# Tying the v maxima and the first weight pass to their emission places, and emitting loads and stores one slot later, in an attention and mixture-of-experts kernel

## The chip, the cores and the metric

One core of one Trainium2 chip runs the whole kernel. The metric is device time in microseconds (us), the median of three runs. TensorE has two clock levels, 1.2 and 2.4 GHz; the profile prints the granted clock as a share of full speed, so 0.5 is the lower level.

## The reference, cut to what matters

Inputs are q, k, v of shape (4 batches, 12 heads, 448 positions, 64), float32; w_in (768 x 2048) and w_out (2048 x 768), float64; and phi (768 x 32), w1 and w2 (8 experts, 768 x 1024 and 1024 x 768) of a second, soft mixture, float32.

```
scores = q k^T / 8, causal mask, softmax (denominator + 1e-9), times v
x = attention output as (1792 tokens, 768)
h = x @ w_in ; g = max(0.01 h, h) ; y = g @ w_out            # first mixture
logits = y @ phi ; d = column softmax ; c = row softmax       # second mixture
slots = d^T y ; per expert: relu(slots w1) w2 ; out = c @ slots_out
```

## The kernel before, in words

**Stages.** The work on attention goes by pairs of heads: 24 pairs n, six to a batch (NP = 6), each in three slots (`attention_slots`, L507). Slot 1 of pair n multiplies P by v for pair n-1 (`attend`, L417, tile O), lowers the maxima, and starts the scores of n; slot 2 has the inverses of the sums (`inverses`, L428, tile rs); slot 3 has `columns` (L452), the last scores, and the transposes of q and k for pair n+2 (`qk_stacks`, L331, tile qkps). `stage` (L736) runs slots: stage 0 has 21 (pairs 0 to 6, attention alone), and three stages of 18 follow, in which one column of g per slot is computed for the batch before (`up`, L583: 18 matmuls into H, then Prelu on ACT, L625). Batches 0 and 1 store g to DRAM (L627). What comes after stage 3 (from some 486 us) is the rest of batch 3, the logits, and the second mixture, whose weights are read from DRAM.

**Weights.** w_in and w_out come as doubles, 16 units each, and are turned into float32 by hand. `load_raw` (L153) loads raw words into a ring of raw buffers (3 in stages 0 to 2, 2 in stage 3; BUFS, L150). `to_f32` (L184) makes two first passes on ACT, Abs of the high word into t (L195) and its Sign into sg (L196), then for w_in a maximum on DVE (L198), and two integer passes on DVE (L199 shifts, L200 reads the low word and t); L200 is the last reader of the raw buffer. After it `load_raw` is called at once, so that the next unit's load is emitted there. t has a ring of 3 in stages 1 and 2, sg of 2. `prep_in` (L207) then finds a scale (`pow2_scale`, L106), and makes two half-precision parts on ACT and POOL (L214 to L224). `prep_out` (L225) multiplies by the sign on POOL (L231), stores the result to DRAM (wsc, L233) and transposes it on TensorE (wt_ps, wp_ps, wf_ps). Units 0 to 5 of w_in are in stage 0, 6 to 15 in stage 1, ten units of w_out in stage 2, the last six in halves in stage 3, spread over the first slots of a stage by `prep_start` (L273).

**v.** `load_v(n)` (L309) loads one pair's v into a ring of VRING = 7; `reduce_v(n)` (L319) takes its absolute maximum on DVE (L325), and after a batch's sixth one, a scale of the batch follows, which `columns` reads. In slot 3 of pair n the kernel emits `load_qk(n + 4)`, `load_v(n + 6)` and `reduce_v(n + 5)`, in this order. v of pair n + 6 takes the buffer that `attend(n - 1)` has read in slot 1 of pair n.

**What sets the order.** TensorE's order is written out: `in_order` (L97) puts each matmul behind the last one emitted. The order on DVE, ACT, POOL and SP (the queue that issues all DMAs) is chosen by the framework when the program is built: it simulates the engines, and on each one takes the instruction of highest priority among those whose inputs are there in the simulation. Priority follows emission, attention 300 places ahead (AHEAD, L740). An instruction whose input comes early in the simulation can so be put far ahead of its place of emission. On the chip each engine then runs its list strictly in order. `tc.issue_after(i)` adds an edge by which what is emitted under it is put behind i on i's engine; raw loads have had one already, behind the last q, k or v load (`last_load`, L164).

Of the kernel before, what the change touches and what calls it, by code (L numbers as in the profile page):

```python
# [10 lines left out]
F32 = mybir.dt.float32  # L11
# [23 lines left out]
def tile_attn_moe_softmoe(ctx: ExitStack, tc: tile.TileContext, q, k, v, w_in, w_out, phi, w1, w2, out, dbg=None):  # L35
    nc = tc.nc
# [55 lines left out]
    chain = [None]  # L92

    def last_tensor():
        return next(i for i in reversed(nc.cur_bb.bb.instructions[-80:]) if i.engine == mybir.EngineType.PE)

# [87 lines left out]
    def to_f32(u, absmax=None):  # L184
# [9 lines left out]
        ti = t.bitcast(I32)  # L194
        nc.scalar.activation(t, hw.bitcast(F32), AF.Abs, scale=2.0**-112)  # L195
        nc.scalar.activation(sg, hw.bitcast(F32), AF.Sign)  # L196
# [3 lines left out]
        nc.vector.scalar_tensor_tensor(ti, lw, 29, ti, ALU.logical_shift_right, ALU.bitwise_or)  # L200
        load_raw()
        return t, sg

    w_in32 = w_in.bitcast(I32)
# [20 lines left out]
    def prep_out(us):  # L225
# [3 lines left out]
        for u in us:  # L229
            wo, sg = to_f32(u)  # L230
            nc.gpsimd.tensor_tensor(wo, wo, sg, ALU.mult)  # L231
            c0 = DH * (u[2] or 0)
            nc.sync.dma_start(  # L233
                wsc.rearrange("(k g a p) n -> k a g p n", k=4, g=4, a=4)[f // 4, f % 4][:, :, c0 : c0 + wo.shape[1]], wo
            )
            yield
# [82 lines left out]
    def reduce_v(n):  # L319

        b, hp = divmod(n, NP)
        if hp == 0:
            v_am[b] = am = const.tile([128, NP + 1], F32, tag="v_am", bufs=2, name=f"v_am{b}")
            nc.vector.memset(am, 0.0)
        nc.vector.tensor_reduce(v_am[b][:CP, hp : hp + 1], v_t[n], AX.XY, ALU.max, apply_absolute_value=True)  # L325
        if hp == NP - 1:
            am = v_am[b]
            nc.vector.tensor_reduce(am[:, NP:], am[:, :NP], AX.X, ALU.max)
            s_v[b], inv_v[b] = pow2_scale(am[:, NP:], f"v{b}")
# [177 lines left out]
    def attention_slots():  # L507
# [10 lines left out]
        for n in range(NPAIR + 1):  # L518
# [14 lines left out]
            if here:  # L533
                weights(n, 1)
            yield
            if n > 0:
# [5 lines left out]
            if n + 2 < NPAIR:  # L542
                qk_stacks(n + 2)
                if n + 4 < NPAIR:
                    load_qk(n + 4)
            if n + NP < NPAIR:
                load_v(n + NP)
            if NP <= n + NP - 1 < NPAIR:
# [187 lines left out]
    def stage(slots, count, columns_of_g=None):  # L736

        had = started[0]
        for x in range(slots):
            with tc.high_priority(offset=AHEAD):  # L740
                next(slots_of_attention, None)
                if columns_of_g is not None and x not in GAPS:
                    next(columns_of_g)
# [296 lines left out]
```

## Time and profile before

| what | us |
|---|---|
| median of three runs | 719.35 |
| lowest, highest | 716.97, 721.56 |
| the profiled execution, and its span | 717.05, 715.3 |
| PE busy (share of span) | 606.0 (85%) |
| DVE, ACT, POOL busy | 354.8, 289.8, 232.2 |
| mean granted clock of TensorE | 0.938 |

The span is the time from the first to the last instruction. PE is TensorE's matmuls, DVE is VectorE, ACT is ScalarE, POOL is GpSimd, SP the queue of DMAs. A busy share is a mean over stages that have different limits; the windows below split it. L12 is line 12 of the kernel; all ordered matmuls have the line of their helper, L99, and are told apart by the tile that they write.

### The profile page before, as it was taken

To read this page: it belongs to the slowest core of one execution; us is meant where nothing else is said; L and a number is where in the kernel's file an instruction comes from. 1 tells how busy PE (TensorE), PEld (TensorE's weight loads), DVE (VectorE), ACT (ScalarE), POOL (GpSimd) and SP (SyncE) were. 2 spreads that over 40 slices of the span, in tenths; PEclk is the share of its full clock that TensorE was granted. 3 is DMA by queue.
4 is the path that set the end of the run, shared out by engine and by line. 5 is a ranking of instruction groups with operands and counts; after the bars stand their busy time and mean duration, and the time that the engine had idled before them with its cause. 6 is when DMAs were issued, how large, how long until landed. Compare 5 with 4: busy or idle time off the path is not lost.

```text
span 715.3 us, 12308 instructions
## 1 busy us (share of the span) xinstructions
PE 606.0 (85%) x4836; PEld 337.4 (47%) x4836; DVE 354.8 (50%) x884; ACT 289.8 (41%) x571; POOL 232.2 (32%) x247
## 2 busy tenths in 40 slices
PE   2888759997988799979799999999998996998544
PEld 2555535554544455546455555554343444454114
DVE  5787645677774446355326666534646423001004
ACT  1677543566764446445245555441122112011003
POOL 4468733567656333335113443331000000000000
PEclk9999977999899899979989999999999998899797
DMA  9933165454345335542213522201989435999967
GB/s 185 260 97 78 40 172 140 110 166 133 114 130 149 127 117 153 151 133 65 78 53 102 152 68 67 68 23 57 378 331 376 154 105 223 426 424 424 423 270 308
DMA packets 102449, 125.67 MB, mean 176 GB/s; under 512 B 69240, under 2 KB 91256, under 8 KB 98296
## 3 DMA queue, kind: packets, MB, share of 16 engines
q1 hardware_dynamic: 102392, 124.89, 52.6%
q8 instruction: 38, 0.62, 0.3%
q14 instruction: 19, 0.16, 0.1%
HBM read 105.74 MB, written 19.14 MB: 175 GB/s over the span
## 4 chain that ended last, share of the span: by engine, by line
PE 49%; DMA 18%; DVE 15%; ACT 8%; issue 4%; POOL 3%; SPq 2%; DVEq 0%; ACTq 0%; POOLq 0%
PE H L99 21%; DMA w<-in_moe_w_dram 8%; PE O L99 6%; DMA v<-in_v_dram 5%; PE T L99 4%; PE g_acc L99 3%; DVE g_nat L565 2%; DVE rs L440 2%; DVE junk L362 2%; PE ph L898 2%; PE qkps L99 2%; DMA raw_i_None<-in_moe_w_in_dram 2%; PE L L99 2%; ACT mr L374 1%; PE wt_ps L99 1%
## 5 line engine op out<-in xcount | busy, mean ns | idle before, releaser
L99 PE MATMUL H<-x,w 128*128 128x448 f16 x1152 | 235.7, 360 | 6.1 <-ACT g L625 6.1
L99 PEld LDWEIGHTS <-w 128*128 128x128 f16 x1152 | 110.6, 100 | 123.7 <-issue 33.3
L362 DVE CUSTOM_DVE_ANT_0 junk<-S,mask 112x448 bf16<-112x448 f32 (+1 forms) x192 | 84.6, 441 | 69.6 <-PE S L99 67.2
L402 POOL TENSOR_SCALAR_AFFINE_SELECT P<-P 112x448 f32<-112x448 f32 x48 | 30.6, 637 | 154.1 <-ACT P L398 154.1
L625 ACT ACTIVATE g<-H,iv 128x448 f32<-128x448 f32 x58 | 36.6, 631 | 102.4 <-PE H L99 95.2
L398 ACT ACTIVATE P<-T 112x672 f32<-112x672 f32 (+1 forms) x72 | 56.9, 790 | 24.8 <-PE T L99 24.6
L99 PE MATMUL T<-qkt 64*112 64x336 f32 (+3 forms) x576 | 60.3, 322 | 5.1 <-ACT P L398 4.4
L99 PE MATMUL O<-P,v 112*64 112x448 f32 (+3 forms) x384 | 58.2, 449 | 5.1 <-POOL P L402 4.7
L440 DVE RECIPROCAL rs<-rs 128x224 f32<-128x224 f32 x36 | 53.3, 1521 | 6.8 <-ACT rs L438 6.8
L99 PEld LDWEIGHTS T<-qkt 64*112 64x112 f32 x576 | 45.8, 187 | 13.7 <-ACT P L398 5.6
L411 POOL TENSOR_TENSOR tsum<-tsum,P 112x448 f32<-112x448 f32 (+1 forms) x48 | 44.8, 934 | 2.6
L99 PEld LDWEIGHTS O<-P,v 112*64 112x64 f32 x384 | 27.6, 151 | 34.7 <-issue 16.5
L374 ACT ACTIVATE mr<-mps,own 128x112 fp32r<-128x112 f32 x96 | 26.0, 354 | 43.7 <-PE mps L99 43.7
L986 PE MATMUL po<-w,hz 128*32 128x384 f32 x256 | 27.5, 551 | 18.2 <-DMA w<-in_moe_w_dram 18.2
L99 PE MATMUL S<-qkt 64*112 64x448 f32 (+1 forms) x192 | 34.0, 395 | 9.2 <-DVE mxe L362 7.3
L407 POOL TENSOR_TENSOR tsum<-P 112x672 f32<-112x672 f32 x24 | 40.1, 1672 | 1.8
L565 DVE STREAM_TRANSPOSE g_nat<-g 128x448 f32<-128x448 f32 x26 | 16.5, 639 | 45.5 <-ACT g L625 45.5
L99 PE MATMUL T<-mr,onesr 64*112 64x448 f32 (+1 forms) x192 | 32.8, 339 | 7.2 <-ACT mr L374 7.1
L215 POOL TENSOR_TENSOR cv_i_None<-cv_i_None,cs_i_None 128x768 f32<-128x768 f32 x16 | 26.8, 1680 | 30.1 <-ACT cs_i_None L214 30.0
L325 DVE TENSOR_REDUCE v_am<-v 112x1 f32<-112x512 f32 x24 | 16.4, 685 | 39.2 <-DMA v<-in_v_dram 39.1
L340 DVE TENSOR_TENSOR qkt<-qkps,qkt 128x448 fp32r<-128x448 f32 x48 | 28.2, 618 | 14.3 <-ACT qkt L339 14.2
L475 POOL TENSOR_TENSOR x<-rs,x 128x448 f16<-128x448 f32 x24 | 26.1, 1088 | 26.6 <-ACT x L474 26.6
(172 smaller groups left out, 842.1 us busy)
## 6 DMA issues: line engine op xcount, KB each, us to landing
w<-in_moe_w_dram SPq DMA_DIRECT2D x32, 1536.0 KB
raw_i_None<-in_moe_w_in_dram SPq DMA_DIRECT2D x16, 768.0 KB
raw_o_None<-in_moe_w_out_dram SPq DMA_DIRECT2D x10, 768.0 KB
g_far<-g SPq DMA_DIRECT2D x32, 224.0 KB
gb<-g_far SPq DMA_DIRECT2D x8, 896.0 KB
wo<-wsc SPq DMA_DIRECT2D x4, 1536.0 KB
qk<-in_q_dram SPq DMA_DIRECT2D x48, 112.0 KB
qk<-in_k_dram SPq DMA_DIRECT2D x48, 112.0 KB
```

The source lines that it names most:

```text
L99: op(*args, **kwargs)
L340: nc.vector.tensor_tensor(st[:, j, 1], p, st[:, j, 0].bitcast(F32), ALU.subtract)
L362: nc.vector.tensor_tensor_reduce(out=junk[:, :w], in0=ps[:, a, at : at + w], in1=mask[:, S - w :], scale=-1.0, scalar=3e38, op0=ALU.add, o ...
L374: nc.scalar.activation(mr[:, i], ps, AF.Copy, scale=own[:, i : i + 1])
L398: nc.scalar.activation(x[:, :, o : o + at], ps[:, :, :at], AF.Exp, scale=SCALE)
L402: nc.gpsimd.affine_select(out=d, in_=d, compare_op=ALU.is_ge, fill=0.0, base=0, pattern=[[0, 4], [1, CP]], channel_multiplier=-1,)
L407: nc.gpsimd.tensor_tensor(tsum[:CP], p[0][:CP, :, 0, CP:], p[0][:CP, :, 1, : S - CP], ALU.add)
L411: nc.gpsimd.tensor_tensor(y, y, p[1][:CP, :, j, : S - CP * (j + 2)], ALU.add)
L440: nc.vector.reciprocal(rs[:, c : c + S // 2], rs[:, c : c + S // 2])
L565: nc.vector.transpose(g_nat[:, :, 32 * f : 32 * (f + n)].rearrange("p c (f x) -> p f c x", x=32), gts[b, f].rearrange("p (c x) -> p c x", ...
L625: nc.scalar.activation(g, ps, AF.Prelu, scale=iv[b][:, f : f + 1], alpha=SLOPE)
L986: nc.tensor.matmul(po[h][32 * g : 32 * g + 32], hp[:, (t0 + t) % 8], wt[:, t, DH * h - c0 : DH * (h + 1) - c0], start=t0 + t < 4, stop=t0 ...
```

## The change: what it does

1. `reduce_v` of batches 1 to 3 is put behind the DVE instruction that was emitted last before it (18 reductions).
2. The Abs pass (L195) of every unit after stage 0 is put behind the ACT instruction emitted last before it. Sign (L196) gets no edge.
3. Raw loads and wsc stores are not emitted where they were, but put on a list `asked`, which the next slot empties first thing, inside the block of raised priority (`ask`).
4. `load_qk(n + 4)` goes to the front of this list in slot 3, and so is emitted at the start of slot 1 of pair n+1; `load_v(n + 6)` goes to its front in slot 2, and so is emitted at the start of slot 3, where it stood near the end.

```diff
--- before.py
+++ after.py
@@ -91,8 +91,11 @@
     TR = [3]
     chain = [None]
 
+    def last_on(engine):
+        return next(i for i in reversed(nc.cur_bb.bb.instructions[-400:]) if i.engine == engine)
+
     def last_tensor():
-        return next(i for i in reversed(nc.cur_bb.bb.instructions[-80:]) if i.engine == mybir.EngineType.PE)
+        return last_on(mybir.EngineType.PE)
 
     def in_order(op, *args, **kwargs):
         with tc.issue_after(chain[0]) if chain[0] is not None else ExitStack():
@@ -192,14 +195,21 @@
         t = pools[stage].tile([128, w], F32, tag="cv_t", bufs=nt, name="cv_" + nm)
         sg = pools[stage].tile([128, w], BF16, tag="cv_s", bufs=ns, name="cs_" + nm)
         ti = t.bitcast(I32)
-        nc.scalar.activation(t, hw.bitcast(F32), AF.Abs, scale=2.0**-112)
+        with tc.issue_after(last_on(mybir.EngineType.Activation)) if stage else ExitStack():
+            nc.scalar.activation(t, hw.bitcast(F32), AF.Abs, scale=2.0**-112)
         nc.scalar.activation(sg, hw.bitcast(F32), AF.Sign)
         if absmax is not None:
             nc.vector.tensor_reduce(absmax, t, AX.X, ALU.max)
         nc.vector.tensor_scalar(ti, ti, 3, None, ALU.logical_shift_left)
         nc.vector.scalar_tensor_tensor(ti, lw, 29, ti, ALU.logical_shift_right, ALU.bitwise_or)
-        load_raw()
+        asked.append(load_raw)
         return t, sg
+
+    asked = []
+
+    def ask():
+        while asked:
+            asked.pop(0)()
 
     w_in32 = w_in.bitcast(I32)
     w_out32 = w_out.bitcast(I32)
@@ -230,9 +240,8 @@
             wo, sg = to_f32(u)
             nc.gpsimd.tensor_tensor(wo, wo, sg, ALU.mult)
             c0 = DH * (u[2] or 0)
-            nc.sync.dma_start(
-                wsc.rearrange("(k g a p) n -> k a g p n", k=4, g=4, a=4)[f // 4, f % 4][:, :, c0 : c0 + wo.shape[1]], wo
-            )
+            rows = wsc.rearrange("(k g a p) n -> k a g p n", k=4, g=4, a=4)[f // 4, f % 4]
+            asked.append(partial(nc.sync.dma_start, rows[:, :, c0 : c0 + wo.shape[1]], wo))
             yield
             if u[2] is None:
                 yield
@@ -322,7 +331,8 @@
         if hp == 0:
             v_am[b] = am = const.tile([128, NP + 1], F32, tag="v_am", bufs=2, name=f"v_am{b}")
             nc.vector.memset(am, 0.0)
-        nc.vector.tensor_reduce(v_am[b][:CP, hp : hp + 1], v_t[n], AX.XY, ALU.max, apply_absolute_value=True)
+        with tc.issue_after(last_on(mybir.EngineType.DVE)) if b else ExitStack():
+            nc.vector.tensor_reduce(v_am[b][:CP, hp : hp + 1], v_t[n], AX.XY, ALU.max, apply_absolute_value=True)
         if hp == NP - 1:
             am = v_am[b]
             nc.vector.tensor_reduce(am[:, NP:], am[:, :NP], AX.X, ALU.max)
@@ -532,6 +542,8 @@
                 maxima(n + 1, TILES[1])
             if here:
                 weights(n, 1)
+            if n + NP < NPAIR:
+                asked.insert(0, partial(load_v, n + NP))
             yield
             if n > 0:
                 columns(n - 1)
@@ -542,9 +554,7 @@
             if n + 2 < NPAIR:
                 qk_stacks(n + 2)
                 if n + 4 < NPAIR:
-                    load_qk(n + 4)
-            if n + NP < NPAIR:
-                load_v(n + NP)
+                    asked.insert(0, partial(load_qk, n + 4))
             if NP <= n + NP - 1 < NPAIR:
                 reduce_v(n + NP - 1)
             yield
@@ -738,6 +748,7 @@
         had = started[0]
         for x in range(slots):
             with tc.high_priority(offset=AHEAD):
+                ask()
                 next(slots_of_attention, None)
                 if columns_of_g is not None and x not in GAPS:
                     next(columns_of_g)
```

## Rows read from the trace of the kernel before

**Rows 1.** Chain of work that ended last (page, part 4): shares by engine, then by line.

```profile
PE 49%; DMA 18%; DVE 15%; ACT 8%; issue 4%; POOL 3%; SPq 2%; DVEq 0%; ACTq 0%; POOLq 0%
PE H L99 21%; DMA w<-in_moe_w_dram 8%; PE O L99 6%; DMA v<-in_v_dram 5%; PE T L99 4%; PE g_acc L99 3%; DVE g_nat L565 2%; DVE rs L440 2%; DVE junk L362 2%; PE ph L898 2%; PE qkps L99 2%; DMA raw_i_None<-in_moe_w_in_dram 2%; PE L L99 2%; ACT mr L374 1%; PE wt_ps L99 1%
```

**Rows 2.** Pair windows: us, busy (count) PE, PEld, DVE, ACT, POOL; clock, DMA.

```profile
57.00:68.00 11.00, 9.38 (x102) 6.28 (x99) 9.21 (x30) 7.80 (x16) 8.55 (x9) 1.00 0.28 63
94.00:112.60 18.60, 13.27 (x93) 10.14 (x93) 11.05 (x29) 9.48 (x16) 6.24 (x7) 0.59 0.72 215
134.60:155.30 20.70, 19.01 (x133) 10.59 (x132) 14.54 (x38) 15.75 (x27) 13.67 (x11) 1.00 0.49 139
197.00:222.00 25.00, 21.77 (x137) 11.46 (x135) 19.23 (x45) 16.59 (x29) 15.75 (x12) 0.93 0.45 128
222.00:246.50 24.50, 18.35 (x109) 9.18 (x104) 8.91 (x22) 9.67 (x17) 8.44 (x9) 0.79 0.44 139
246.50:265.90 19.40, 19.16 (x138) 11.04 (x137) 10.50 (x30) 8.13 (x18) 7.81 (x9) 1.00 0.45 129
265.90:289.20 23.30, 22.17 (x180) 13.12 (x179) 13.40 (x28) 13.43 (x28) 9.97 (x8) 1.00 0.50 147
289.20:314.70 25.50, 20.21 (x154) 12.19 (x153) 11.82 (x26) 13.18 (x28) 8.66 (x9) 0.88 0.46 144
314.70:339.60 24.90, 24.37 (x175) 14.04 (x175) 11.58 (x26) 11.83 (x27) 10.55 (x10) 0.91 0.30 83
339.60:368.20 28.60, 23.59 (x168) 14.40 (x167) 8.89 (x23) 9.90 (x23) 5.65 (x7) 0.88 0.28 74
466.30:486.30 20.00, 19.61 (x153) 10.61 (x155) 6.85 (x9) 8.32 (x20) 7.52 (x9) 1.00 0.07 20
```

**Rows 3.** Costliest groups (page, part 5), the v maxima: busy, mean ns | idle before.

```profile
L325 DVE TENSOR_REDUCE v_am<-v 112x1 f32<-112x512 f32 x24 | 16.4, 685 | 39.2 <-DMA v<-in_v_dram 39.1
```

**Rows 4.** DVE in order of time: start, us, what [idle before <-releaser].

```profile
72.41 0.69 DVE L325 TENSOR_REDUCE v_am<-v 112x1 f32<-112x512 f32 x1 [1.27 <-DMA v<-in_v_dram]
...
204.54 0.69 DVE L325 TENSOR_REDUCE v_am<-v 112x1 f32<-112x512 f32 x1 [2.36 <-DMA v<-in_v_dram]
...
234.85 0.69 DVE L325 TENSOR_REDUCE v_am<-v 112x1 f32<-112x512 f32 x1 [7.13 <-DMA v<-in_v_dram]
...
301.71 0.69 DVE L325 TENSOR_REDUCE v_am<-v 112x1 f32<-112x512 f32 x1 [8.41 <-DMA v<-in_v_dram]
...
324.78 0.69 DVE L325 TENSOR_REDUCE v_am<-v 112x1 f32<-112x512 f32 x1 [4.02 <-DMA v<-in_v_dram]
...
352.69 0.69 DVE L325 TENSOR_REDUCE v_am<-v 112x1 f32<-112x512 f32 x1 [9.06 <-DMA v<-in_v_dram]
```

**Rows 5.** SP's queue around the last load of v, in order of time.

```profile
342.69 2.02 SPq L312 DMA_DIRECT2D v<-in_v_dram  x1
```

**Rows 6.** PE in order of time: the stalls over 3 us from 100 to 360 us.

```profile
104.37 1.01 PE L99 MATMUL rb<-r,first 128*64 128x112 f32 x8 [3.29 <-DVE r L450]
...
238.11 2.40 PE L99 MATMUL H<-x,w 128*128 128x448 f16 x6 [3.81 <-ACT g L625]
...
309.24 0.53 PE L99 MATMUL S<-qkt 64*112 64x224 f32 x2 [3.22 <-DVE mxe L362]
...
358.63 0.90 PE L99 MATMUL wt_ps<-ident,cv_o_None 128*128 128x128 f32 x3 [4.74 <-ACT wprime L259]
```

**Rows 7.** ACT in order of time: first passes, and what one v maximum delays.

```profile
101.68 0.89 ACT L195 ACTIVATE cv_i_None<-raw_i_None 128x768 f32<-128x768 f32 x1 [2.87 <-DMA raw_i_None<-in_moe_w_in_dram]
...
236.66 0.88 ACT L196 ACTIVATE cs_o_None<-raw_o_None 128x768 bf16<-128x768 f32 x1 [8.33 <-DMA raw_o_None<-in_moe_w_out_dram]
...
266.59 0.93 ACT L195 ACTIVATE cv_o_None<-raw_o_None 128x768 f32<-128x768 f32 x1
...
357.40 0.56 ACT L474 CAST x<-rs 128x448 f16<-128x448 f32 x1 [6.75 <-DVE rs L473]
```

**Rows 8.** SP's queue: the raw load that the Sign of 236.66 waits for.

```profile
227.69 1.96 SPq L172 DMA_DIRECT2D raw_o_None<-in_moe_w_out_dram  x2
```

**Rows 9.** Durations of DVE's last conversion pass, L200: ns min/median/max.

```profile
L200 DVE SCALAR_TENSOR_TENSOR cv_o_None<-raw_o_None,cv_o_None x10: 887/960/2945, 208.7 to 335.2; 128x768 int32<-128x768 int32 x10
```

**Rows 10.** Costliest groups (page, part 5), a POOL pass over one unit: busy, mean ns | idle before.

```profile
L215 POOL TENSOR_TENSOR cv_i_None<-cv_i_None,cs_i_None 128x768 f32<-128x768 f32 x16 | 26.8, 1680 | 30.1 <-ACT cs_i_None L214 30.0
```

## The prediction

> **What bounds the kernel now.** I read the chain of work that ended last first. TensorE holds 49% of it, DVE 15%, and one transfer stands out among its lines, the load of v with 5% of a 715.3 us span, some 36 us [rows 1]; w with its 8% is the stream of weights at the end, which the change does not touch. So TensorE is the bound in most places, and what is to be had lies where it stands still.
>
> The windows, cut at the starts of successive attentions (one pair of heads each), show where that is [rows 2]. In stage 3 the pair from 466.3 takes 20.00 us, 19.61 of it TensorE at full clock: nothing to gain there. In stage 1 an undisturbed pair takes 20.7 us (from 134.6), and in stage 2, which has the transposes of w_out besides, two take 19.4 and 23.3, a mean of 21.35. But the three from 289.2 take 25.5, 24.9 and 28.6 us, with the granted clock at 0.88, 0.91 and 0.88. The pair from 222 (24.5 us) has the lowest clock of these, 0.79; the one across the stage boundary at 94 takes 18.6 us where one of stage 0 takes 11.0.
>
> What fits the three bad windows is on DVE. The maxima of v take 685 ns each and leave DVE idle 39.1 us in front of them [rows 3], 31 of them in five stalls of 2.36, 7.13, 8.41, 4.02 and 9.06 us between 202 and 353 us [rows 4]. DVE runs its list in order, so the reciprocals, the rs products and the masked maxima queued behind a v maximum all wait. The rs product of 357 us comes late, and ACT waits 6.75 us for it [rows 7]; ACT's next copies are then late too, and TensorE waits 4.74 us. The same happens through the masked maxima at 309 us: 3.22 us [rows 6].
>
> **Is the load late, or the maximum early?** The last v is issued at 342.69, and DVE starts on it at 352.69 [rows 4, 5]. By the code its buffer is given back by the attention of pair 16, which starts the window at 339.6; no issue much earlier is possible. But its maximum is emitted only in slot 3 of pair 18, one to two pairs later, and nobody needs it before the batch's scale. The simulated transfer is evidently shorter than the 10 us seen here, so the maximum was put some 30 us ahead of its place. That is what the edge forbids.
>
> **The change part by part.**
>
> *v maxima, 18 with an edge.* Removed: the waits. Each maximum now stands behind slot 3 of its pair, at least one pair (20.7 us) after its load was emitted, twice the longest transfer in the rows (10 us, issue to start). Gain in the three bad windows: 25.5 + 24.9 + 28.6 = 79.0 against 3 x 21.35 = 64.05, so 15 us. Ends: the two stalls alone (3.22 + 4.74 = 8.0), and, from above, those plus the clock that the windows lost (0.12 x 25.5 + 0.09 x 24.9 + 0.12 x 28.6 = 8.7), 16.7; I take 15, since the window comparison holds both. Their 18 x 0.69 us of work stays. The scale of a batch now follows its last maximum by less, with one pair left until `columns` reads it: nothing; without that cover, 3 x 0.69 = 2 us. Stage 0 loses little (1.27 us the longest stall there, [rows 4]): nothing, 1.3 at most.
>
> *The pair from 222.* Two waits lie side by side: DVE's for v (7.13, until 234.85) and ACT's for raw_o (8.33, until 236.66), after which TensorE goes on, 3.81 us late [rows 4, 6, 7]. The pair is 24.5 - 20.7 = 3.8 us long. The ACT wait is a Sign, which gets no edge. I take half, 1.9; ends 0 and 3.8 + 0.21 x 24.5 = 8.9.
>
> *Abs with an edge.* At the boundary ACT waits 2.87 us for the first raw unit of stage 1, DVE then waits for ACT, and TensorE stands 3.29 us for a reciprocal that is behind this on DVE [rows 6, 7]. With Abs at its place, DVE's passes leave the front of the list. Sign can still be put there, but no DVE pass follows from it alone. I take the 3.29; ends 0 and 18.6 - 11.0 = 7.6. The pair from 197 (25.0, 4.3 over its kind) has conversions in front of attention on all engines; Abs at its place thins them out. I take 1.5; ends -2 (they only move) and 4.3.
>
> *Loads and stores a slot later.* A slot is 20.7 / 3 = 6.9 us. Rings of three raw buffers and about 1.4 slots per unit leave some three slots between a load and its first pass, so Abs is covered. q, k and v go ahead of raw in the list, and SP's queue has as many instructions as before (the same DMAs). wsc stores a slot later hold t longer, in a ring of three: nothing, since three units are over four slots. Sign is the unknown: today one stands 30 us ahead of its unit's Abs (236.66 against 266.59) and 9 us behind its load (227.69) [rows 7, 8]. sg has two buffers, so a Sign waits for the unit two before, whose Abs is now later; that brings Sign back too, but not all the way. I charge 3 us for new waits; ends 0 and one such wait in full, 8.3.
>
> *Moved integer passes.* L200 takes 887 ns at least, 960 in the median and 2945 at most [rows 9], so most of them meet nothing. I charge nothing; if all 20 units of stages 1 and 2 took the longest, 20 x 1.99 = 40 us of DVE, of which its 15% of the chain [rows 1] would be 6; a gain is at most the one long pass, 0.3. The Trainium skill, page "SBUF — State Buffer", section "Who interferes with whom", says that a DVE instruction with two inputs in SBUF is blocked for the whole of a GpSimd instruction that reads SBUF, and that a tensor_reduce never is. The long pass agrees, and by that rule each L200 that moves under a POOL pass pays for it: with POOL busy 13.67 of 20.7 us in stage 1, an estimate of half a 1.68 us pass [rows 10] for two thirds of 20 units is 11 us of DVE and 1.6 of the sum, which would then be 702.
>
> **The sum.** -15 - 1.9 - 3.3 - 1.5 + 3 = -18.7. The profiled execution took 717.05 (span 715.3, 1.75 around it); the changed one should take 698.4. The median of the runs lies 2.3 above the profiled one, so I say 700. What ends last after that is TensorE itself, with 20 to 21 us a pair. The tail from 486 us is the same work and comes earlier by what was saved.
>
> **Rivals.**
>
> *Sign takes the wait over.* Without its edge, Sign goes to where its raw load lands in the simulation, and with loads a slot later, ACT waits where DVE did. For it: 8.33 us at 228. Against it: the ring of two. The v gain then counts half: 7.5 + 1.9 of the rest, 717.05 - 9.4 = 708, median 710. Chance 0.18.
>
> *Slower: ACT blocked again and again.* The same mechanism, where it decides. The measured block of 8.33 us made its pair 3.8 us longer. 17 units of stages 1 and 2 have their load behind a first pass (all but the first three). If every second one of them lands behind its Sign, 8 x 3.8 = 30 against 18.7 + 3 gained: 726 profiled, 728. The point is some 9 us between load and Sign (227.69 to 236.66): with less than that ACT waits, and from six such blocks the gain is gone. Against it: with Abs held back, sg and the load are both tied to the unit's slot. Chance 0.07.
>
> *All of it.* Every pair from 112.6 to 368.2 runs undisturbed: 6 x 20.7 + 5 x 21.35 = 231 where 255.6 are spent, so 24.6, and the boundary gives 7.6: 685, median 687. For it: the clock lost in so many windows is given back with the stalls. Against it: conversions still share DVE and ACT with attention. Chance 0.10.
>
> *Nothing.* The edges end at an instruction that itself stands early, or the three windows are long for the transposes of w_out and not for v: within 1%, 717. Against it: TensorE's idle time in them is named. Chance 0.05.
>
> **How the numbers follow.** The forecast has 0.60; its own range is 690 to 710, from the ends of the v term and of the two Abs terms. The range of 8 in 10 reaches from the third rival to the first and beyond it to the start of "nothing": 684 to 715. 1% is 7.2 us (712.2 is the bound), about what a measurement of this kernel can tell from no change. Faster by over 1%: 0.57 of the forecast, 0.11 of the first rival and the 0.10 of the third, 0.78. Within 1%: 0.03 of the forecast, 0.06 of the first rival, the 0.05 of "nothing", and 0.01 of the slower case, 0.15. Slower: 0.01 of the first rival and 0.06, 0.07.
>
> **What the changed profile would show.** Right: DVE's idle time before the v maxima from 39.1 to under 5 us, all of it early; the three windows at 20 to 23 us with the clock at 1.00; no v load in the chain after 100 us; Abs and Sign of a unit closer together than 30 us. Wrong: ACT's idle time before Sign on raw_o or raw_i, 8.3 us for full units now, at 20 or more; the H matmuls waiting for w from POOL, because conversions start too late; or a window of 25 us or more in stage 2 with no DVE wait for v in it.

## The result, and the profile after: 1.0% slower

The changed kernel takes 723.44 us (median of 9 runs, 722.44 to 727.95), the kernel before 716.97 in the 9 runs beside it (713.99 to 721.56): ratio 1.0102, 95% interval 1.0074 to 1.0129. I had said 700, range 684 to 715. The profiled execution took 726.06, its span is 724.4.

The page's chain of the kernel after, shares by engine and then the lines that matter, answers to [rows 1]. In the changed kernel the helper of the ordered matmuls is L102, Abs L199, Sign L200, the maximum of w (w_am) L202, the v maximum L335.

```profile
PE 45%; DMA 15%; DVE 14%; ACT 10%; POOL 7%; issue 5%; SPq 2%; ACTq 0%; DVEq 0%; POOLq 0%
PE H L102 20%; DMA w<-in_moe_w_dram 8%; PE T L102 3%; PE O L102 3%; DVE rs L450 3%; PE g_acc L102 3%; DMA raw_i_None<-in_moe_w_in_dram 3%; DMA raw_o<-in_moe_w_out_dram 3%; DVE g_nat L575 2%; POOL cv_i_None L225 2%; ACT mr L384 2%; PE dn L102 2%; PE ph L909 2%; PE L L102 2%; DMA raw_o_None<-in_moe_w_out_dram 1%
```

The 5% of v are gone. In their place stand raw words (3, 3 and 1%, where one line of 2% was listed) and POOL at 7%, where it had 3%. So the transfer that I meant to take off the path was taken off it, and the weights' conversion came onto it.

The windows of the same kernel, cut as in [rows 2] (us, busy and count of PE, PEld, DVE, ACT, POOL; clock, DMA share, GB/s): the boundary, the last three pairs of stage 1, the three pairs of stage 2 that were to gain, and the pair behind them.

```profile
97.30:115.20 17.90, 9.94 (x99) 6.60 (x99) 9.49 (x28) 8.43 (x17) 10.47 (x11) 0.98 0.70 197
181.20:215.00 33.80, 25.16 (x134) 14.07 (x133) 20.67 (x51) 17.41 (x30) 19.79 (x16) 0.80 0.42 121
215.00:234.90 19.90, 19.05 (x134) 10.73 (x133) 14.64 (x38) 14.06 (x25) 10.41 (x9) 1.00 0.39 112
234.90:250.90 16.00, 14.87 (x112) 8.42 (x111) 7.58 (x20) 8.29 (x16) 6.96 (x7) 1.00 0.37 104
295.20:317.10 21.90, 18.86 (x152) 11.12 (x150) 11.55 (x26) 12.75 (x27) 9.31 (x9) 0.97 0.56 167
317.10:343.10 26.00, 23.40 (x178) 13.71 (x175) 11.54 (x26) 13.85 (x29) 9.64 (x10) 0.96 0.46 138
343.10:365.30 22.20, 21.63 (x168) 12.74 (x167) 11.74 (x26) 11.36 (x25) 8.87 (x8) 1.00 0.38 97
365.30:388.10 22.80, 17.19 (x128) 9.94 (x127) 6.90 (x19) 7.91 (x19) 3.42 (x4) 0.85 0.25 76
```

The three pairs take 21.9 + 26.0 + 22.2 = 70.1 us where they took 79.0. The clock there is 0.96 to 1.00 where it was 0.88 to 0.91 [rows 2]. But one pair of stage 1 is now 33.8 us long, and the last pair of stage 2 takes 22.8. In the kernel before, the boundary and these two pairs, cut at the same attentions, are

```profile
89.60:112.60 23.00, 14.82 (x102) 10.64 (x101) 12.21 (x31) 11.23 (x20) 10.56 (x11) 0.66 0.67 194
171.70:196.80 25.10, 22.20 (x136) 12.22 (x135) 19.55 (x47) 15.51 (x28) 17.75 (x15) 0.86 0.48 139
368.20:384.20 16.00, 15.73 (x128) 9.50 (x127) 6.89 (x19) 7.01 (x17) 3.41 (x4) 1.00 0.10 38
```

so 8.7 and 6.8 us are lost in the two pairs. The two pairs behind the one of 33.8 us are shorter than before: 19.9 and 16.0 us, where they took 24.3 and 25.4 (cut at 196.8, 221.1 and 246.5; the rows of [rows 2] from 197 and 222 are cut almost a microsecond late). The boundary's row in [rows 2] starts in the middle of an attention; cut alike it fell from 23.0 to 17.9 us. But the pairs in front of it take 66.9 us (30.4 to 97.3, clock 0.85) where they took 58.4 (31.2 to 89.6, clock 1.00), and attention 6, which starts stage 1, comes at 115.2 instead of 112.6.

The waits of the kernel after (who <- for what: us in all, times, longest), those on the lines of the change:

```profile
PE w_ps L113 <- DVE w_am L202: 12.9, 6, 3.2
PE v_ps L113 <- DVE v_am L338: 10.3, 4, 5.9
DVE v_am L335 <- DMA v<-in_v_dram: 3.8, 5, 1.3
ACT cs_o L200 <- DMA raw_o<-in_moe_w_out_dram: 22.9, 10, 6.2
DVE w_am L202 <- ACT cv_i_None L199: 28.5, 10, 5.9
```

DVE's wait for v fell from 39.1 [rows 3] to 3.8. Two waits are new in kind or size: TensorE stands 12.9 us at w_ps (0.5 before), and ACT stands 22.9 us at Sign for half units of w_out (12.9 before; whole units, 8.3 before, now 2.7). w_ps and v_ps are the small matmuls of `pow2_scale` (L113): they spread a column of maxima over the partitions, they go straight to `nc.tensor.matmul`, and so they are the only matmuls of the stages whose place on TensorE is chosen by the framework. Of the 10.3 us at v_ps, 5.9 are the first batch's, at 17 us; the kernel before waits 6.9 there.

### The profile page after: what moved, and what is told of

It is laid out like the page before. It is cut to its first block, busy times and chain, and to the rows that moved or that the text cites. A ratio compares the mean times of both kernels' runs of the same rounds, so it can differ in the third digit from the quotient of the medians.

```text
span 724.4 us, 12305 instructions
## 1 busy us (share of the span) xinstructions
PE 605.1 (84%) x4836; PEld 338.1 (47%) x4836; DVE 350.2 (48%) x884; ACT 290.2 (40%) x571; POOL 230.7 (32%) x247
## 4 chain that ended last, share of the span: by engine, by line
PE 45%; DMA 15%; DVE 14%; ACT 10%; POOL 7%; issue 5%; SPq 2%; ACTq 0%; DVEq 0%; POOLq 0%
PE H L102 20%; DMA w<-in_moe_w_dram 8%; PE T L102 3%; PE O L102 3%; DVE rs L450 3%; PE g_acc L102 3%; DMA raw_i_None<-in_moe_w_in_dram 3%; DMA raw_o<-in_moe_w_out_dram 3%; DVE g_nat L575 2%; POOL cv_i_None L225 2%; ACT mr L384 2%; PE dn L102 2%; PE ph L909 2%; PE L L102 2%; DMA raw_o_None<-in_moe_w_out_dram 1%
## 5 line engine op out<-in xcount | busy, mean ns | idle before, releaser
L102 PE MATMUL H<-x,w 128*128 128x448 f16 x1152 | 233.9, 358 | 0.0
L102 PEld LDWEIGHTS <-w 128*128 128x128 f16 x1152 | 109.7, 99 | 117.0 <-issue 25.7
L412 POOL TENSOR_SCALAR_AFFINE_SELECT P<-P 112x448 f32<-112x448 f32 x48 | 29.1, 607 | 145.8 <-ACT P L408 145.6
L408 ACT ACTIVATE P<-T 112x672 f32<-112x672 f32 (+1 forms) x72 | 56.9, 790 | 23.3 <-PE T L102 22.8
L102 PE MATMUL T<-qkt 64*112 64x336 f32 (+3 forms) x576 | 60.4, 322 | 5.6 <-ACT P L408 4.5
L102 PE MATMUL O<-P,v 112*64 112x448 f32 (+3 forms) x384 | 58.4, 447 | 4.2 <-POOL P L412 4.1
L102 PEld LDWEIGHTS T<-qkt 64*112 64x112 f32 x576 | 45.8, 186 | 13.5 <-ACT P L408 5.7
L102 PEld LDWEIGHTS O<-P,v 112*64 112x64 f32 x384 | 27.0, 148 | 35.7 <-issue 18.7
L102 PE MATMUL T<-mr,onesr 64*112 64x448 f32 (+1 forms) x192 | 33.1, 341 | 12.6 <-ACT mr L384 12.6
L997 PE MATMUL po<-w,hz 128*32 128x384 f32 x256 | 25.4, 514 | 20.7 <-DMA w<-in_moe_w_dram 20.7
L575 DVE STREAM_TRANSPOSE g_nat<-g 128x448 f32<-128x448 f32 x26 | 16.5, 639 | 49.5 <-ACT g L635 49.5
L102 PE MATMUL S<-qkt 64*112 64x448 f32 (+1 forms) x192 | 34.0, 396 | 6.8 <-ACT P L408 3.9
```

Of the source, the lines that this page charges most:

```text
L102: op(*args, **kwargs)
L408: nc.scalar.activation(x[:, :, o : o + at], ps[:, :, :at], AF.Exp, scale=SCALE)
L412: nc.gpsimd.affine_select(out=d, in_=d, compare_op=ALU.is_ge, fill=0.0, base=0, pattern=[[0, 4], [1, CP]], channel_multiplier=-1,)
L575: nc.vector.transpose(g_nat[:, :, 32 * f : 32 * (f + n)].rearrange("p c (f x) -> p f c x", x=32), gts[b, f].rearrange("p (c x) -> p c x", ...
```

## The experiments

The three parts of the change were mixed, and two mends were added: an edge on Sign, and a written place for w_ps. V is the edge on the v maximum, A the edge on Abs, D the later emission (raw loads, q/k/v loads, stores). The diffs are cut to the lines that matter: those of e1 to e3, e11, e13 and e15 are against the kernel before, that of e16 against e3, the others against the changed kernel. Ratios are to the kernel before, run beside each, with their 95% interval. What differs after a first reading of the traces is the price of A (theory A), of D (theory B), and of Sign, which keeps its old place while its raw words come later (theory S).

**The parts alone.**

e1: only V.

```diff
+        with tc.issue_after(last_on(mybir.EngineType.DVE)) if b else ExitStack():
             nc.vector.tensor_reduce(v_am[b][:CP, hp : hp + 1], v_t[n], AX.XY, ...)
```

> Only the edge on the 18 v maxima is kept; Abs has no edge and loads and stores are emitted where they were. Theory A (the edge on Abs is what costs: the first pass comes late, the maximum of a w_in unit after it, and TensorE, which runs its list in order, stands at the scale's matmul w_ps): the v waits of DVE fall from 39 to under 5 us, TensorE waits for w_am as little as before (0.5 us), and the time is 700 to 710. Theory B (the later loads cost, by waits of ACT for raw words): also faster, 700 to 710. Theory C (the v wait was covered by something else all along, and any of the edges only moves it): 714 to 720.

707.99 us, 0.9867 (0.9829 to 0.9906). The windows of the three pairs are 21.5 + 24.6 + 22.4 = 68.5, so 10.5 less than before. DVE's wait fell to 11.4 us, not under 5: one of 8.8 is left, at 231.7 us in stage 1. The whole stage 2, attention 12 to attention 18, of e1, and then of the kernel before, as windows:

```profile
242.50:369.90 127.40, 120.92 (x929) 71.20 (x928) 62.03 (x152) 63.27 (x136) 46.12 (x44) 0.99 0.40 114
```

```profile
246.50:384.20 137.70, 125.22 (x931) 74.28 (x930) 63.08 (x152) 63.47 (x136) 46.06 (x44) 0.94 0.36 104
```

PE's busy time fell 4.3 us for the same 930 matmuls, with the clock at 0.99 instead of 0.94; the other 6 us of the 10.3 are standstill. The edge has a price of its own, seen on PE in order of time (start, duration, what, [idle before <- releaser]):

```profile
114.99 0.77 PE L113 MATMUL v_ps<-ident,v_am 128*128 128x128 f32 x2 [7.23 <-DVE v_am L338]
```

All waits of v_ps are 14.8 us in e1 and 6.9 before, of which the first batch's at some 18 us is 7.1 and 6.9; the rest is new: the batch's scale now follows its last maximum late, and TensorE comes to it first.

e2: only A.

```diff
+        with tc.issue_after(last_on(mybir.EngineType.Activation)) if stage else ExitStack():
             nc.scalar.activation(t, hw.bitcast(F32), AF.Abs, scale=2.0**-112)
```

> Only the edge on Abs is kept. Theory A: the v waits stay (30 us or more), TensorE waits 8 to 15 us for w_am at w_ps in stage 1, and the time is 722 to 732. Theory B: ACT's waits for raw words are those of before (about 27 us in all), w_ps waits little, 712 to 720. Theory C: 714 to 720.

717.98 us, 1.0005 (0.9973 to 1.0037): no change in sum, against theory A's time. Attention 6, the first of stage 1, starts at 109.1 instead of 112.6, about the 3.3 us of the prediction. The wait that theory A names is there:

```profile
PE w_ps L113 <- DVE w_am L202: 10.3, 6, 3.2
```

Before, w_ps waited for w_am once, 0.5 us. Yet stage 1 as a whole is no longer than before (133.4 us, and 133.9): its last two pairs take 20.8 and 15.0 us in e2 and give back what w_ps costs.

e3: only D (raw loads and stores on the list, q, k and v at its front).

```diff
-        load_raw()
+        asked.append(load_raw)
...
-                    load_qk(n + 4)
+                    asked.insert(0, partial(load_qk, n + 4))
```

> Only the later emission of loads and stores is kept, no edges. Theory A: within 1% of before, 712 to 723, with the v waits of before. Theory B: ACT waits 10 us or more longer for raw words than before, and the time is 723 to 733. Theory C: 714 to 720.

731.74 us, 1.0185 (1.0144 to 1.0227), 13.4 us where I had charged 3. Stage 2 of e3 as one window takes 151.3 us, 13.6 more than before:

```profile
245.10:396.40 151.30, 126.57 (x929) 74.01 (x929) 64.87 (x155) 66.69 (x141) 46.84 (x45) 0.92 0.39 113
```

ACT of e3 in order of time has two long waits there, and TensorE stands behind each:

```profile
297.22 0.88 ACT L200 ACTIVATE cs_o_None<-raw_o_None 128x768 bf16<-128x768 f32 x1 [7.21 <-DMA raw_o_None<-in_moe_w_out_dram]
...
328.50 0.88 ACT L200 ACTIVATE cs_o_None<-raw_o_None 128x768 bf16<-128x768 f32 x1 [9.01 <-DMA raw_o_None<-in_moe_w_out_dram]
```

```profile
299.13 0.72 PE L102 MATMUL T<-mr,onesr 64*112 64x448 f32 x2 [6.21 <-ACT mr L384]
...
330.40 0.71 PE L102 MATMUL T<-mr,onesr 64*112 64x448 f32 x2 [8.02 <-ACT mr L384]
```

The queue of SP, in order of time, tells why. First e3, then the kernel before, around the load for which the first of these Signs waits:

```profile
283.11 0.52 SPq L212 DMA_DIRECT2D wsc<-cv_o_None  x1
285.55 1.37 SPq L312 DMA_DIRECT2D qk<-in_q_dram  x2
286.97 2.48 SPq L312 DMA_DIRECT2D qk<-in_k_dram  x2
289.55 2.11 SPq L175 DMA_DIRECT2D raw_o_None<-in_moe_w_out_dram  x1
```

```profile
281.07 0.33 SPq L172 DMA_DIRECT2D raw_o_None<-in_moe_w_out_dram  x1
281.49 0.38 SPq L627 DMA_DIRECT2D g_far<-g  x1
282.75 0.52 SPq L233 DMA_DIRECT2D wsc<-cv_o_None  x1
285.19 1.42 SPq L303 DMA_DIRECT2D qk<-in_q_dram  x2
```

Before, the raw load stands ahead of a g store, a wsc store and the next pair's q and k. In e3 it stands behind all of them. Counted from the start of the stage it is issued at 44.5 us instead of 34.6, and the one after it (320.11 in e3, 307.49 before) at 75.0 instead of 61.0. Sign stands where it stood and waits.

**Two parts together.** Each takes one part out of the change.

e4: V and D.

```diff
-        with tc.issue_after(last_on(mybir.EngineType.Activation)) if stage else ExitStack():
+        with ExitStack():
             nc.scalar.activation(t, hw.bitcast(F32), AF.Abs, scale=2.0**-112)
```

> The changed kernel without the edge on Abs: v edge and later loads. Theory A: the waits of TensorE for w_am at w_ps (12.9 us in the changed kernel) fall below 3, and the time is 703 to 714. Theory B: 718 to 728, with ACT waiting for raw words as in the changed kernel (some 25 us). Theory C: 715 to 722.

725.83 us, 1.0101 (1.0066 to 1.0135), against theory A: without A the change takes as long as with it.

e5: V and A.

```diff
-        asked.append(load_raw)
+        load_raw()
...
-                    asked.insert(0, partial(load_qk, n + 4))
+                    load_qk(n + 4)
```

> The changed kernel with loads and stores where they were: both edges, no later emission. Theory S (what costs is the later emission together with a Sign that has no edge: the raw load comes a slot later on SP's queue, Sign stays near its old place in ACT's list, and ACT stands in front of the scores' work): ACT waits under 20 us for raw words, none of them over 6 us in front of a full unit's Sign in stage 2, and the time is 704 to 713, that of the v edge alone (708) give or take the edge on Abs (no effect alone). Theory A (the edge on Abs costs by waits of TensorE at w_ps): 715 to 722.

716.46 us, 0.9986 (0.9955 to 1.0016). That is theory A's range. V gives 1.3% alone and nothing beside A: stage 1 takes 135.3 us here and 126.8 in e1, and e5 has 12.6 us of w_ps waits there (0.3 in e1). ACT's Sign waits on half units are 21.3 us (12.4 in e1), but all lie in stage 3, which is not longer than in e1.

e6: A and D.

```diff
-        with tc.issue_after(last_on(mybir.EngineType.DVE)) if b else ExitStack():
+        with ExitStack():
             nc.vector.tensor_reduce(v_am[b][:CP, hp : hp + 1], v_t[n], AX.XY, ...)
```

> The changed kernel without the edge on v: Abs edge and later emission. If the parts add up (v alone -10, Abs 0, later emission +13): 729 to 735. If the edge on Abs takes part of the later emission's cost away (by holding sg, and so Sign, back): 722 to 729, with the two waits of TensorE for mr of 6 and 8 us that the later emission alone has in stage 2 gone. The v waits of DVE are back, 30 us or more.

728.0 us, 1.0149 (1.0113 to 1.0184). The two waits for mr are gone, and a new one of 5.4 us stands at the end of stage 2. The interval meets that of D alone, so that A takes part of D's price is likely, not shown.

| V | A | D | ratio | product of the parts |
|---|---|---|---|---|
| x | | | 0.9867 | |
| | x | | 1.0005 | |
| | | x | 1.0185 | |
| x | x | | 0.9986 | 0.9872 |
| x | | x | 1.0101 | 1.0050 |
| | x | x | 1.0149 | 1.0190 |
| x | x | x | 1.0102 | 1.0055 |

The last column multiplies the ratios of the single parts. The largest gap, 1.1%, is that of V with A.

The profiled executions by stage (us; attentions 6, 12 and 18 start stages 1, 2 and 3; e7 and e12 follow below):

| | before attention 6 | stage 1 | stage 2 | from attention 18 on |
|---|---|---|---|---|
| before | 112.6 | 133.9 | 137.7 | 331.1 |
| the change | 115.2 | 135.6 | 137.2 | 336.3 |
| e1 (V) | 115.7 | 126.8 | 127.4 | 336.2 |
| e2 (A) | 109.1 | 133.4 | 136.7 | 337.5 |
| e3 (D) | 115.4 | 129.7 | 151.3 | 333.9 |
| e5 (V and A) | 113.3 | 135.3 | 131.0 | 333.0 |
| e7 (the change, Sign tied) | 111.0 | 135.5 | 127.1 | 333.0 |
| e12 (V, A, Sign tied, w_ps in order) | 110.3 | 125.3 | 127.0 | 332.2 |

Each row is one execution, and executions of the kernel before lie up to 7.6 us apart, so 2 or 3 us in one column show little. V alone gains 7.1 us in stage 1 and 10.3 in stage 2. With A beside it the gain of stage 1 is gone; with D besides, that of stage 2 as well.

**What A and D do to Sign and to the scale.**

e7: the change, and Sign with the same edge as Abs.

```diff
-        nc.scalar.activation(sg, hw.bitcast(F32), AF.Sign)
+        with tc.issue_after(last_on(mybir.EngineType.Activation)) if stage else ExitStack():
+            nc.scalar.activation(sg, hw.bitcast(F32), AF.Sign)
```

> The changed kernel with an edge on Sign as well, behind the ACT instruction emitted last before it, which is its own unit's Abs. Theory S: ACT's waits for raw words fall from some 29 us to under 10, TensorE's wait of 5.5 us for mr at the start of stage 3 goes, and the time is 710 to 718. Theory A (w_ps waits of TensorE, which stay here): 720 to 728.

708.75 us, 0.9869 (0.9844 to 0.9894), better than theory S had put it. The raw waits of ACT go from 34 us in the changed kernel (22.9 + 4.6 + 3.8 + 2.7) to one line in the waits of e7; w_ps stays:

```profile
PE w_ps L113 <- DVE w_am L203: 12.3, 5, 3.2
ACT cv_i_None L199 <- DMA raw_i_None<-in_moe_w_in_dram: 3.5, 3, 1.9
```

Stage 2 falls from 137.2 to 127.1 us, stage 1 stays (135.6 and 135.5). So the untied Sign costs stage 2; that w_ps costs stage 1 is tested in e9.

e8: V, and an edge on Sign in place of that on Abs, no D.

```diff
-        with tc.issue_after(last_on(mybir.EngineType.Activation)) if stage else ExitStack():
-            nc.scalar.activation(t, hw.bitcast(F32), AF.Abs, scale=2.0**-112)
-        nc.scalar.activation(sg, hw.bitcast(F32), AF.Sign)
+        nc.scalar.activation(t, hw.bitcast(F32), AF.Abs, scale=2.0**-112)
+        with tc.issue_after(last_on(mybir.EngineType.Activation)) if stage else ExitStack():
+            nc.scalar.activation(sg, hw.bitcast(F32), AF.Sign)
```

> The v edge, and an edge on Sign (behind its own unit's Abs) but none on Abs; loads and stores where they were. Theory S: the 10.5 us that ACT waits at one Sign in stage 2 with the v edge alone (TensorE 8.0 behind it) goes, and the time is 698 to 705. If Abs, free to be early, takes the wait over: 705 to 711.

702.84 us, 0.9791 (0.9749 to 0.9833). Abs, left free, does not take the wait over: ACT waits 7.5 us for raw words in all (4.9 + 2.6). So the first pass to be held back is Sign, the one whose result is needed last; Abs, behind which DVE and TensorE wait, may stay early.

e9: the change, with the scale matmuls of w units after stage 0 in TensorE's written order.

```diff
-        nc.tensor.matmul(ps, absmax.to_broadcast([128, 128]), ident, start=True, stop=True)
+        matmul = mm if name[0] == "w" and int(name[1:]) >= EARLY[0] else nc.tensor.matmul
+        matmul(ps, absmax.to_broadcast([128, 128]), ident, start=True, stop=True)
```

> The changed kernel with one edit: the matmul of the scale of a w_in unit (w_ps, units 6 to 15) joins the written order of TensorE, so that it stands behind the attention and the g column of the slot after its unit's Abs, and not where the simulation saw the maximum done. Theory A (the edge on Abs costs because TensorE stands at w_ps for a maximum that now comes late): the waits of TensorE for w_am fall from 12.9 us to under 4, stage 1 (attention 6 to 12, 135.6 us in the changed kernel) takes 122 to 129, and the time is 711 to 718. Rival (DVE and ACT are late in stage 1 for the conversions themselves, and w_ps only shows it): the wait moves to H or to the scores, stage 1 stays above 132 us, and the time is 720 to 726.

716.5 us, 0.9981 (0.9952 to 1.001), in theory A's range. Stage 1 falls from 135.6 to 129.6 us, less than I had hoped, for TensorE still waits 8.2 us at w_ps (its line is now that of the helper):

```profile
PE w_ps L102 <- DVE w_am L203: 8.2, 4, 4.5
```

e10: the change with the edits of e7 and e9.

> The changed kernel with both mends: the edge on Sign (708.8 alone) and w_ps in the written order. If the two costs are separate: 708.8 less what the written order gives by itself, 694 to 703, with ACT's waits for raw words under 10 us and TensorE's for w_am under 4. If the written order gives nothing: 705 to 712.

701.69 us, 0.9762 (0.9734 to 0.9791), 22 us under the changed kernel, so the two costs are separate. With Sign held back too, w_ps waits 3.9 us:

```profile
PE w_ps L102 <- DVE w_am L204: 3.9, 3, 1.4
ACT cv_i_None L200 <- DMA raw_i_None<-in_moe_w_in_dram: 4.7, 5, 2.4
```

e12: as e10, without D.

> All three edges (v, Abs, Sign) and w_ps in the written order, with loads and stores where they were in the kernel before. If the later emission costs only through Sign: the same as with it, 694 to 703. If it costs more besides (raw loads in front of q, k and v): 5 us or more faster than with it. If it gives something with all first passes tied: 5 us or more slower.

699.05 us, 0.9739 (0.9712 to 0.9765), the lowest median of all; the interval meets that of e10, so D costs little, if anything, once Sign is tied. The waits of w_ps are as in e10 and ACT hardly waits for raw words at all; then stage 2 as a window:

```profile
PE w_ps L102 <- DVE w_am L204: 3.8, 3, 1.3
ACT cv_i_None L200 <- DMA raw_i_None<-in_moe_w_in_dram: 0.9, 3, 0.6
```

```profile
235.60:362.60 127.00, 120.74 (x929) 71.18 (x928) 64.95 (x158) 69.40 (x144) 50.29 (x47) 0.99 0.47 135
```

**What in D costs.** Theory E: the edge by which each raw load is put behind the last q, k or v load emitted, in place in both kernels, drags raw loads behind the next pair's q and k, once these stand at the front of the list.

e11: of D only the raw loads.

```diff
-        load_raw()
+        asked.append(load_raw)
```

> The kernel before with only the raw loads emitted a slot later (no edges; q, k, v loads and wsc stores where they were). Theory S (a Sign without an edge stands in front of a raw load that is a slot late): this is nearly all of the later emission's cost (+13 with all of it): 725 to 733, with waits of ACT of 6 to 9 us at Signs of full units in stage 2. If the q, k and v loads or the stores carry the cost: 714 to 721.

717.01 us, 0.9986 (0.9963 to 1.0009). A raw load a slot later costs nothing by itself, against theory S in its simple form. In SP's queue of e11 the load stands alone again, ahead of q and k:

```profile
304.74 0.33 SPq L175 DMA_DIRECT2D raw_o_None<-in_moe_w_out_dram  x1
```

e13: raw loads and q, k, v loads, stores in place.

```diff
-        load_raw()
+        asked.append(load_raw)
...
+            if n + NP < NPAIR:
+                asked.insert(0, partial(load_v, n + NP))
...
-                    load_qk(n + 4)
+                    asked.insert(0, partial(load_qk, n + 4))
-            if n + NP < NPAIR:
-                load_v(n + NP)
```

> The kernel before with raw loads and q, k and v loads emitted as in the change, stores where they were, no edges. Theory E (the cost of the later emission comes from both together: a raw load has an edge behind the last q, k or v load emitted, and that is now the load of the next pair's q and k, which SP holds until TensorE has transposed; raw loads of stage 2 then stand one or two places later on SP's list, in front of Signs that have not moved): 727 to 735, with the two long waits of TensorE for mr in stage 2. If the stores carry it: 714 to 721.

731.28 us, 1.0188 (1.0149 to 1.0227): the whole of D, without the stores.

e15: only q, k and v loads.

```diff
+            if n + NP < NPAIR:
+                asked.insert(0, partial(load_v, n + NP))
...
-                    load_qk(n + 4)
+                    asked.insert(0, partial(load_qk, n + 4))
-            if n + NP < NPAIR:
-                load_v(n + NP)
```

> The kernel before with only the q, k and v loads emitted as in the change; raw loads and stores where they were, no edges. Theory E: SP's list in stage 2 is that of before, 714 to 721. If the q, k and v loads by themselves carry the cost (later q and k): 725 to 735.

713.79 us, 0.9952 (0.9925 to 0.9979), half a per cent faster. Neither half costs anything, the two together 13 us.

e16: e3 without that edge.

```diff
-            with tc.issue_after(last_load[0]):
+            with ExitStack():
                 if kind == "i":
```

> The later emission alone (731.7 us) without the edge that puts a raw load behind the last q, k or v load. Theory E: the two long waits of TensorE for mr in stage 2 (6.2 and 8.0 us) go or shrink under 3 us, and the time is 714 to 723. If the edge has no part in it: 727 to 735.

720.67 us, 1.0023 (0.999 to 1.0055). Stage 2 as one window is as before:

```profile
251.70:388.50 136.80, 125.59 (x931) 74.41 (x930) 62.96 (x153) 63.58 (x136) 45.86 (x44) 0.94 0.35 100
```

SP's queue of e16, in order of time, first in stage 0 and then in stage 2:

```profile
23.49 1.29 SPq L175 DMA_DIRECT2D raw_o<-in_moe_w_out_dram  x2
...
286.31 0.33 SPq L175 DMA_DIRECT2D raw_o_None<-in_moe_w_out_dram  x1
```

The raw load that stood at 34.6 us of stage 2 before, and at 44.5 in e3, is at 34.6 again, and the one at 61.0 before is at 61.0 again (312.75). So the edge, with the new order of the list, is shown to be the cause of D's price in stage 2. Stage 0 is 10.6 us longer (attention 6 starts at 123.2 us instead of 112.6): without the edge four loads of half units, which belong to stage 3, go out at 23.49 and 32.27 us, and ACT, DVE and POOL start on them there; the pair that takes 13.2 us before (31.2 to 44.4) takes 21.4 (30.2 to 51.6). Stage 1 gives 5.4 back.

## Why the prediction was wrong

**"Loads and stores a slot later ... I charge 3 us; ends 0 and one such wait in full, 8.3": failed.** D alone costs 13.4 us, more than the upper end, and beside V and A some 8.3 (0.9986 without it, 1.0102 with it). I wrote that q, k and v go ahead of raw in the list and that SP's queue has as many instructions as before. Both hold, and what follows was not drawn: the raw load has an edge behind the last of them (`last_load`, L164, told of in the description of the kernel), SP works its list in order, and q and k wait for a buffer. The load moves by 10 and 14 us, not by a slot of 6.9. I had the Sign as "the unknown", with 9 us between load and Sign [rows 7, 8], and the right point: with less, ACT waits. In e3 ACT waited twice, 7.21 and 9.01 us, and the two waits behind it on TensorE, 6.21 and 8.02, make 14.2 us, the size of the stage's 13.6. The ring of two did not bring Sign back in e3, where Abs is free. Where Abs has its edge, it did so for whole units, as I had argued: their Signs wait 2.4 us in e6 and 2.7 in the change, 16.5 in e3. What D costs in the change is another Sign, that of the first half unit, below.

**"Abs with an edge": 3.3 + 1.5 gained: failed; the term that I left out is the wait at w_ps, 12.9 us.** Alone (e2), the boundary gave 3.5; in the change attention 6 starts 2.6 us later than before, not 3.3 earlier. An edge that forbids a pass to come early lets everything behind it come late. Abs feeds w_am on DVE, and w_am feeds w_ps on TensorE. I costed Abs only by what it stood in front of, and never followed its readers: w_ps has no place in the written order, so the framework puts it where w_am is done in its simulation, and on the chip TensorE, in order, waits there. PE of the changed kernel in order of time (see the windows: two of these are in the pair of 33.8 us):

```profile
148.94 0.80 PE L113 MATMUL w_ps<-ident,w_am 128*128 128x128 f32 x2 [3.22 <-DVE w_am L202]
...
195.98 0.49 PE L113 MATMUL w_ps<-ident,w_am 128*128 128x128 f32 x2 [3.22 <-DVE w_am L202]
...
207.52 0.80 PE L113 MATMUL w_ps<-ident,w_am 128*128 128x128 f32 x2 [2.92 <-DVE w_am L202]
```

That is the stall I had found for v, moved from DVE to TensorE. The pair with two of them takes 33.8 us instead of 25.1. With w_ps in the written order stage 1 is 6.0 us shorter (e9).

**"The pair from 222", 1.9 (0 to 8.9), and the 1.5 of the pair from 197: right in sign, far too small.** The pair from 222 takes 16.0 us instead of 25.4, and the one from 197 19.9 instead of 24.3. Of the two waits that lay side by side in the pair from 222, DVE's for v is 1.35 us there now, and no Sign waits for raw words. It is A that does this, not V: the two pairs take 20.8 and 15.0 us in e2 but 23.0 and 25.0 in e1, where one Sign still waits 10.5 us and TensorE 8.0 behind it. So A gives about as much in stage 1 as w_ps takes there: 133.4 us in e2, 133.9 before.

**"*v maxima*, 15 us; ends 8.0 and 16.7": right in its mechanism, and 10.5 in size.** The three pairs gave 10.5 us in e1, and e1 is 1.3% faster. What was mis-sized is the middle pair, which kept 24.6 of its 24.9 us: I took 21.35 as what every pair of stage 2 should take. I also left out stage 1, where V alone gains 7.1. In the changed kernel the three gave 8.9, and the pair behind them lost 6.8 of it (16.0 to 22.8) at the Sign of the first half unit: ACT and then PE of the changed kernel,

```profile
371.64 0.54 ACT L200 ACTIVATE cs_o<-raw_o 128x384 bf16<-128x384 f32 x1 [6.18 <-DMA raw_o<-in_moe_w_out_dram]
```

```profile
374.17 0.71 PE L102 MATMUL T<-mr,onesr 64*112 64x448 f32 x2 [5.52 <-ACT mr L384]
```

This is D's price again, in the other direction: the edge of these raw loads ends at the last q and k loads emitted, and with D these are the ones of a pair earlier. SP's queue of the changed kernel, and of e5, which has no D:

```profile
365.07 3.25 SPq L175 DMA_DIRECT2D raw_o<-in_moe_w_out_dram  x2
```

```profile
381.94 11.65 SPq L175 DMA_DIRECT2D raw_o<-in_moe_w_out_dram  x3
```

With the load, Sign too moves ahead, into stage 2, and ACT stands there for it. Without D (e5) or with Sign tied (e7) this pair takes 15.9 us.

**"The scale of a batch now follows its last maximum by less ...: nothing; without that cover 2 us": failed.** I looked at the reader of the scale, `columns`, and not at the matmul between. v_ps stands on TensorE's list where the simulation has the maximum done; it cost 7.23 us at one place in e1, and 3.91 there in the change.

**"Moved integer passes: nothing": right.** L204, which was L200, over ten units of w_out (ns min/median/max), answers to [rows 9]:

```profile
L204 DVE SCALAR_TENSOR_TENSOR cv_o_None<-raw_o_None,cv_o_None x10: 895/959/1487, 264.1 to 356.1; 128x768 int32<-128x768 int32 x10
```

The median is the same and the longest is shorter; the mean fell from 1235 to 1092 ns, and over the units of w_in from 1123 to 1110. The Trainium skill's rule of the page "SBUF — State Buffer", section "Who interferes with whom", by which I had estimated 11 us of DVE, would show as longer passes; some long ones are there (1487 ns here, 2278 in w_in), but no more than before, and DVE's busy time fell from 354.8 to 350.2 us.

**The rivals.** What happened is in part the first rival's mechanism (Sign takes the wait over: 34.0 us of raw waits on ACT, 26.8 before), with a time near the second's, and A's cost at w_ps beside it, which no rival had. Tying Sign as well gives 14.7 us back (e7), and putting w_ps in order 7 (e9); 22 together (e10; by the ratios, which set each beside its own runs of the kernel before, 17, 9 and 24). That the second rival came near in time is luck: its condition, every second unit, did not come true. In the change one Sign of a half unit cost TensorE 5.5 us in stage 2. In e3 two Signs of whole units waited long (a third 0.3 us), not eight, and they cost TensorE 6 and 8 us, not the 3.8 that I took from the pair at 222. There v's stall lay beside Sign's; that this had already paid half of the price is likely, since without it (e1) TensorE waits 8.0 us behind the same Sign.

**The signs that I named.** Of the right ones came DVE's idle time before the v maxima (3.8 us) and a chain without v. Of the wrong ones came a window of 25 us or more in stage 2 without a DVE wait for v (26.0) and more waiting at Sign (29.4 us in all, 21.2 before), but at half units.

**What stays open.** V beside D gives less than alone (measured 1.0101, product 1.0050): e4's waits for raw words on whole units are 17.6 us in four, those of e3 16.5 in three, which does not account for it. Stores alone were not run; e3 and e13 differ by 0.0003, so they cost nothing in company, within some 0.4%. v_ps still waits 10.4 us in e12, but 6.7 of these are the first batch's; putting the others in the written order was not tried. Whether A gives anything once Sign is tied is not shown: e8, without A and without the written order, is at 0.9791, and its interval meets that of e12. From attention 18 on, the change, e1 and e2 take 5 to 6 us longer than the kernel before; no run says why.

## What to carry to other kernels

Before an instruction is held back by an edge, follow its readers to the engine that is the bound, and look for one whose place on that engine's list nobody has written: it goes where the builder's simulation believes the input to be ready, and the engine stands there. Of several first readers of a load, tie first the one whose result is needed last: here Sign alone was enough beside V (0.9791), and Abs alone was not (0.9986). When loads change their order on a queue, look at edges between them and write out the queue's list: two moves that cost nothing each cost 13 us together here, because one is tied to the other.

## What the runs showed of the hardware beyond that

A good part of the gain came with the clock: over stage 2, 930 matmuls took 125.2 us of PE time before, at a granted clock of 0.94, and 120.9 in e1 and 120.7 in e12, at 0.99. In the pair of 33.8 us with its two stalls of some 3 us at w_ps the clock was 0.80. So in these rows a microsecond of standstill on TensorE went with a further loss: in stage 2 of e1, 10.3 us were won, of which 4.3 are shorter matmuls.
